# Attention block on one core: the opening rebuilt, from the loads to the first scores

## The chip, the core and the metric

The kernel runs on one core of a Trainium2 chip. The core has five engines with queues of their own: TensorE (PE in the profile; its weight loads are PEld), VectorE (DVE), ScalarE (ACT), GpSimd (POOL) and SyncE (SP), which here only issues DMAs. An engine takes its instructions in the order in which they were written; engines wait for each other by semaphores. TensorE writes its results to PSUM, eight banks of 128 partitions x 512 f32, which VectorE and ScalarE read. The metric is the device time of one execution in microseconds (us).

## The reference

Self-attention on x of 2048 x 448 with 16 heads of 28 channels, in bf16:

```python
qkv = (x @ wqkv).reshape(B, S, 3, H, Dh) ...   # B 1, S 2048, D 448, H 16, Dh 28
q, k, v = qkv[0], qkv[1], qkv[2]
scores = jnp.einsum("bhqd,bhkd->bhqk", q, k) * (Dh ** -0.5)
p = _softmax(scores, axis=-1)
o = jnp.einsum("bhqk,bhkd->bhqd", p, v)
return o (heads joined) @ wo
```

The bulk is the exponential of 16 x 2048 x 2048 scores and the two matmuls on either side of it.

## The kernel before

**Tiling.** Heads go in 4 groups `g` of 4, each head padded to 32 partitions, so a group fills 128. Queries go in 4 chunks `c` of 512, keys in 16 tiles of 128. One group and one chunk make a *set*; there are 16. A set has 4 x 16 = 64 *half-tiles* of scores, 128 keys x 512 queries of one head.

**Two ways to exponentiate.** ScalarE takes two half-tiles at once from a pair of banks (`a0` or `a1`) and writes the tile `pt` (line 802); ten `pt` tiles go round. VectorE takes one half-tile from bank `d0` or `d1` and forms bits of bf16 numbers by adding a constant (`I`, line 817). Four such are a chain; two more operations over the chain add further constants (`J`, line 840), and three terms together, the second and third with copies of V scaled by constants (`VS`, line 466), approximate the exponential. Three chains go round. PV (line 900) multiplies `pt`, `I` and `J` with V into bank `o`, one set at a time. Every exponential is taken of a score less a bound for its query, which comes from the norm of that query times the largest norm of the keys; the bound travels as a spare row of Q and a row of ones in K.

**What is needed before the first scores.** x is loaded in 4 blocks of 512 rows (`xs`), transposed on TensorE in pieces of 128 x 112 (line 508) and copied to `XT`, one half by VectorE (515), one by ScalarE (517). Then, for the first group, K of each block is projected (line 230, 16 matmuls), squared (244), summed by head with a matrix of ones (`blockK`, line 310), and the maximum over keys taken (315). Q of the first chunk is projected and squared too, and its norm summed (381). A root by bit shifts (321, 386, 389) and a join (394) give `QA0`, from which the first scores (621) are made. Only then may the first exponential run. K is copied to `KA` by ScalarE (259) or VectorE (262). V of the first two groups is projected in pairs of key tiles (445) and copied to `VA` (454 ScalarE, 456 VectorE).

**Zero rows.** Q of a set is also laid out in two tiles `QP` of 128 partitions with zeros at the other heads' rows, so that two heads fit one matmul. There are 16 such tiles; the old kernel clears them by 16 DMAs from a tile of zeros (line 539), issued by SP in the opening. `VA` and `WO` are cleared by GpSimd (161, 163), which then issues the 16 loads of `WO` (166).

**The order.** The order on each engine is written by a planner when the kernel is built. It holds a list of operations for each of PE, ACT, DVE and SP with an estimated duration, what they need, which bank they acquire (`acq`) and release (`rel`) and a priority (`pri`, smaller first), and a clock `free` for each engine; it advances the engine whose clock is least and lets it take the best operation that is ready. The landing times of the loads are constants in it (lines 528 to 530). `do_s` places a pair of half-tiles for ScalarE and, where a `d` bank is free (`d_banks`), half-tiles for VectorE. `pick_pe` decides between scores, PV (`do_pv`), listed operations, and matmuls of zeros as a filler. The planner's estimates fix the order alone; at run time the semaphores decide.

**Banks.** `a0` and `a1` are two banks each, `d0`, `d1`, `o` and `m` one. In the main part `m` serves all projections, norms and output projections.

The old opening takes the transposed blocks through `a0` and `a1`, each block a pair of banks and one tile `XT`; the loads of the Q and V weights are issued by ScalarE from within its copies of blocks 1 and 2:

```python
def evac(hf):
    ...
        nc.scalar.copy(out=dst, in_=src)
        if b == 1:
            load_w(0, nc.scalar)
        if b == 2:
            load_w(2, nc.scalar)
```

## Time and profile before

| what | us |
|---|---|
| three runs | 380.9, 380.94, 385.8; median 380.94 |
| profiled execution | 381.23 |
| its span on the core | 379.2 |
| ScalarE busy | 359.0 (95%), 400 instructions |
| TensorE busy | 346.4 (91%) |
| VectorE busy | 341.9 (90%) |
| GpSimd busy | 20.0 (5%) |
| exponentials on ScalarE (line 802) | 376, 345.6 busy |
| half-tiles on VectorE (line 817) | 272, 180.0 busy |
| granted clock of TensorE | 0.999 |

376 exponentials of two half-tiles and 272 single ones make the 1024 half-tiles. Rows of a timeline give start, length, engine, line, operation, output and inputs, shapes, how many instructions were merged and, in brackets, how long the engine stood idle before and what released it. Rows of groups give, behind the bar, busy us and mean ns of one, and then the idle time before them. A mean length contains the overlap with the next instruction, so spacing of starts is the better measure of a stream. The span is counted on the core; the profiled execution's own time has 2.0 us more around it.

### The profile page before, as it was taken

How to read it: one execution, taken by the hardware profiler on the slowest of the kernel's cores; microseconds unless marked ns; L12 is line 12 of the kernel's file. 1: busy time of each engine (PE TensorE's matmuls, PEld its weight loads, DVE VectorE, ACT ScalarE, POOL GpSimd, SP SyncE). 2: the span in 40 equal slices, each digit the busy share in tenths (PEclk: the TensorE clock that was granted, in tenths of full speed). 3: DMA queues.
4: the chain of work that ended last, by engine and by line, in shares of the span. 5: the costliest groups of instructions: out<-in, count | busy, mean ns of one | idle time of the engine just before them, and what ended most of it. 6: DMA issues, size and time to landing. Idle time of an engine off the chain costs nothing.

```text
span 379.2 us, 8747 instructions
## 1 busy us (share of the span) xinstructions
PE 346.4 (91%) x3442; PEld 113.3 (30%) x3462; DVE 341.9 (90%) x655; ACT 359.0 (95%) x400; POOL 20.0 (5%) x47
## 2 busy tenths in 40 slices
PE   7879999999999999999789999989889899989974
PEld 3443322222333233232222222222222222222222
DVE  2499998999999999999899899899999999999943
ACT  2779999999999999999999999999999999999992
POOL 8830000000000000000000000000000000000000
PEclk9999999999999999999999999999999999999999
DMA  8930001011100000011000001000000011110101
GB/s 251 246 102 16 3 19 38 3 41 28 41 6 15 18 3 29 14 28 40 4 30 7 25 15 41 28 31 2 28 5 4 28 39 42 37 43 12 56 14 48
DMA packets 16082, 14.03 MB, mean 37 GB/s; under 512 B 6077, under 2 KB 13609, under 8 KB 16041
## 3 DMA queue, kind: packets, MB, share of 16 engines
q1 hardware_dynamic: 13704, 11.18, 9.8%
q10 hardware_dynamic: 1824, 1.89, 1.8%
q8 instruction: 27, 0.44, 0.5%
q0 software_dynamic: 512, 0.40, 0.5%
q14 instruction: 15, 0.11, 0.1%
HBM read 7.37 MB, written 1.96 MB: 25 GB/s over the span
## 4 chain that ended last, share of the span: by engine, by line
ACT 56%; PE 22%; issue 9%; DMA 6%; DVE 4%; SPq 2%; ACTq 0%; DVEq 0%
ACT pt L802 54%; PE a L621 9%; PE o L900 6%; PE m L230 3%; DMA rr<-scr 3%; PE m L445 2%; DMA WRAW<-in_wqkv_dram 2%; SPq L359 2%; DVE I L817 1%; DMA QP<-zero 1%; DVE QA L353 1%; DVE J L840 1%; DMA den<-o_sb 1%; ACT sq L244 0%; ACT XT L517 0%
## 5 line engine op out<-in xcount | busy, mean ns | idle before, releaser
L802 ACT ACTIVATE pt<-a 128x1024 bf16<-128x1024 f32 x376 | 345.6, 1183 | 1.5 <-PE d L621 1.1
L817 DVE TENSOR_SCALAR I<-d 128x512 int16<-128x512 f32 x272 | 180.0, 682 | 8.0 <-PE d L621 6.6
L621 PE MATMUL a<-QP,KA 32*128 32x512 bf16 (+1 forms) x742 | 144.9, 380 | 18.2 <-ACT pt L802 17.0
L900 PE MATMUL o<-pt,VA 128*32 128x512 bf16 x752 | 106.5, 385 | 0.5 <-ACT pt L802 0.5
L621 PEld LDWEIGHTS <-KA 32*128 32x128 bf16 (+1 forms) x1024 | 52.6, 91 | 155.8 <-issue 153.6
L621 PE MATMUL d<-QP,KA 32*128 32x512 bf16 x267 | 92.6, 384 | 0.2 <-DVE I L817 0.2
L840 DVE TENSOR_SCALAR J<-I 128x2048 int16<-128x2048 int16 x136 | 90.1, 684 | 0.4
L900 PE MATMUL o<-J,VS 128*32 128x512 bf16 x544 | 74.4, 385 | 0.3
L900 PE MATMUL o<-I,VA 128*32 128x512 bf16 x272 | 65.9, 385 | 0.6 <-issue 0.5
L230 PE MATMUL m<-XT,WRAW 112*32 112x512 bf16 x464 | 35.5, 384 | 0.5 <-ACT XT L517 0.3
L900 PEld LDWEIGHTS <-VA 128*32 128x32 bf16 x1024 | 23.9, 94 | 37.0 <-issue 36.7
L900 PEld LDWEIGHTS <-VS 128*32 128x32 bf16 x544 | 16.5, 94 | 16.4 <-issue 16.4
L445 PE MATMUL m<-WRAW,XT 112*128 112x224 bf16 x112 | 15.4, 261 | 0.0
L230 PEld LDWEIGHTS <-WRAW 112*32 112x32 bf16 x512 | 8.4, 94 | 16.0 <-issue 12.9
L445 PEld LDWEIGHTS <-XT 112*128 112x128 bf16 x128 | 10.2, 97 | 7.8 <-issue 6.3
L262 DVE TENSOR_SCALAR KA<-m,kmask,ones 128x512 bf16<-128x512 f32 x13 | 10.4, 803 | 2.1 <-ACT sq L244 1.9
L353 DVE TENSOR_SCALAR QA<-m,qmask 128x512 bf16<-128x512 f32 x15 | 11.1, 742 | 0.5 <-PE m L230 0.5
L515 DVE COPY XT<-a 112x1024 bf16<-112x1024 bf16 x4 | 2.8, 692 | 9.4 <-ACT XT L517 7.8
L651 PE MATMUL o<-zero 128*128 128x512 bf16 x29 | 10.0, 384 | 1.3 <-issue 1.3
L481 PE MATMUL m<-WO,xs 128*128 128x448 bf16 x36 | 11.0, 359 | 0.0
L951 DVE TENSOR_TENSOR xs<-o_sb,rr 128x512 bf16<-128x512 f32 x12 | 8.2, 683 | 2.5 <-DMA rr<-scr 2.5
L929 DVE COPY o_sb<-o 128x512 f32<-128x512 f32 x15 | 10.3, 685 | 0.1
(104 smaller groups left out, 155.0 us busy)
## 6 DMA issues: line engine op xcount, KB each, us to landing
rr<-scr SPq DMA_DIRECT2D x15, 256.0 KB
QP<-zero SPq DMA_DIRECT2D x16, 128.0 KB
QP<-QA SPq DMA_DIRECT2D x60, 28.0 KB
out_dram<-osb SPq DMA_DIRECT2D x14, 112.0 KB
xs<-in_x_dram SPq DMA_DIRECT2D x3, 448.0 KB
WRAW<-in_wqkv_dram ACTq DMA_DIRECT2D x3, 392.0 KB
QP<-su SPq DMA_DIRECT2D x30, 2.0 KB
xs<-in_x_dram ACTq DMA_DIRECT2D x1, 448.0 KB
```

The lines of the kernel that those rows point to most:

```text
L230: nc.tensor.matmul(out=ps[HP * i:HP * (i + 1), :], lhsT=WRAW[t][:, cc, h * Dh:h * Dh + HP], rhs=XT[c][:, cc, :], start=(cc == 0), stop=(cc ...
L262: nc.vector.tensor_scalar(out=KAt[(g, sc)][:], in0=src, scalar1=kmask[:, 0:1], scalar2=ones[:, 0:1], op0=ALU.mult, op1=ALU.add)
L353: nc.vector.tensor_scalar(out=t[:], in0=held[key][:, 0:QW], scalar1=qmask[:, 0:1], scalar2=None, op0=ALU.mult)
L445: nc.tensor.matmul(out=held[key][:, part * w:(part + 1) * w], lhsT=XT[b][:, cc, t * P:(t + 1) * P], rhs=WRAW[2][:, cc, h * w:(h + 1) * w], ...
L481: nc.tensor.matmul(out=held[key][:, 0:D], lhsT=otile(g, c)[:, tq * P:(tq + 1) * P], rhs=WO[:, g, :], start=(g == 0), stop=(g == G - 1))
L621: nc.tensor.matmul(out=out_ap, lhsT=KAt[(g, j // XB)][r, (j % XB) * P:(j % XB + 1) * P], rhs=q[r, :], start=True, stop=True, tile_position ...
L651: nc.tensor.matmul(out=cur["o"][:], lhsT=zero[:, 0:P], rhs=zero[:], start=False, stop=False, skip_group_check=True)
L802: nc.scalar.activation(out=pt[:], in_=ps[:], func=ACT.Exp, scale=LN2 / 128.0)
L817: nc.vector.tensor_scalar(out=dst, in0=pd[:], scalar1=BIAS, scalar2=0.0, op0=ALU.add, op1=ALU.max)
L840: nc.vector.tensor_scalar(out=r[:, w], in0=ch["I"][:, w], scalar1=float(SHIFT[k]), scalar2=None, op0=ALU.add)
L900: nc.tensor.matmul(out=o[HP * i:HP * (i + 1), :], lhsT=vt[:, gg, j % XB, HP * i:HP * (i + 1)], rhs=e["ap"], start=(SETMM[key] == 1), stop= ...
L929: nc.vector.tensor_copy(out=st["o_sb"][:], in_=o[:])
```

## The change

- The first x block is loaded in two halves, by SP and by ScalarE's queue; the Q and V weights are loaded by SP right behind the x blocks. No load is issued from within a copy any more.
- Each transposed block is two tiles `XT{b}_0` and `XT{b}_1` of two pieces each, through two separate banks (`d0`, `d1` or `o`, `m`). ScalarE copies the first half, VectorE the second.
- The 16 zero-row DMAs are replaced by memsets: eight by VectorE in the setup, eight by GpSimd after the join. GpSimd's clearing of the second half of `VA` and of `WO`, and the loads of `WO`, also move behind the join; GpSimd becomes an engine of the planner.
- `k_first` replaces `k_job` and `kn_first` for the first group. Banks: K0 in `a0`, K1 in `a1`, K2 in `d1`, K3 in `o`; norms in the second half of `a0` and `a1`, in `a0`, and in `m`. K0 and K1 are copied by ScalarE, and squared from the copy in SBUF, by GpSimd and by VectorE; K2 and K3 are squared by ScalarE from PSUM and copied by VectorE only after the join. The copy of the first Q and the first scaling of its norm move from VectorE to ScalarE.
- V pairs of the first set all go through bank `m`, none through `o`; they, and every other operation of low priority on `m`, wait for the last norm of K.
- In the main part, `m` may serve as a third bank for VectorE's half-tiles while no operation that wants it is ready within 1 us; and in the first set a ready listed operation goes ahead of PV.

```diff
-    XT = [big.tile([CK, CC, QW], BF16, name=f"XT{b}") for b in range(NXB)]
+    XT = [[big.tile([CK, CC // 2, QW], BF16, name=f"XT{b}_{k}") for k in range(2)] for b in range(NXB)]
...
-    load_x(0, nc.sync)
+    load_x(0, nc.sync, 0, 2)
+    load_x(0, nc.scalar, 1, 2)
     load_w(1, nc.scalar)
     load_x(1, nc.sync)
     load_x(2, nc.scalar)
     load_x(3, nc.sync)
+    load_w(0, nc.sync)
+    load_w(2, nc.sync)
...
+    for c in range(NQC):
+        for k in range(2):
+            nc.vector.memset(QP[c][k][0][:], 0.0)
...
+    for b in range(NXB):
+        clear_v(0, b)
...
+        if op.acq == "m" and op.pri > 5 and ("KN0", NQC - 1) not in evt:
+            return None
...
+    def k_first(sc, bank, nbank, eng, sq_eng, pri, late=False):
+        key = ("K", 0, sc)
+        nkey = ("KN0", sc)
+        last = sc == NQC - 1
+        uses = 1 + (sq_eng == "ACT") + (nbank is None)
...
+        def sq():
+            if sq_eng == "ACT":
+                act_square(key, kmask)
+            else:
+                t = new_sq(key)
+                (nc.gpsimd if sq_eng == "POOL" else nc.vector).tensor_tensor(
+                    out=t[:], in0=KAt[(0, sc)][:], in1=KAt[(0, sc)][:], op=ALU.mult)
...
+        add("PE", CC * D_WAVE + 0.02, mm, pri=pri, cols=448 * CC, acq=bank,
+            need=[("XT", sc, 0), ("XT", sc, 1), ("W", 1)], gives=[key + (0,)])
+        add(eng, 0.72 if eng == "DVE" else 0.72, evac, need=[key + (0,)] + ([("QA", 0, 0)] if late else []), gives=[key],
+            rel=rel, pri=5 if late else pri)
...
             if first:
-                nc.vector.tensor_scalar(out=t[:], in0=held[key][:, 0:QW], scalar1=qmask[:, 0:1], scalar2=qoff[:, 0:1],
-                                        op0=ALU.mult, op1=ALU.add)
+                nc.scalar.activation(out=t[:], in_=held[key][:, 0:QW], func=ACT.Identity, bias=qoff[:, 0:1],
+                                     scale=qmask[:, 0:1])
...
+        def scaled():
+            held["z0"] = wk.tile([P, QW], BF16, name="z", bufs=1)
+            nc.scalar.mul(out=held["z0"][:], in_=held.pop("qn0")[:, 0:QW], mul=MARG ** 4)
...
+    def xt_job(b, banks, pri):
+        def tr(hf):
+            held[("xt", b, hf)] = bank_tile(banks[hf])
...
-    for n, t in (("x", 0), 5.4), (("W", 1), 5.6), (("x", 1), 7.2), (("x", 2), 9.0), (("x", 3), 10.3), \
-            (("W", 0), 13.0), (("W", 2), 14.8):
+    for n, t in (("x", 0), 5.0), (("W", 1), 6.3), (("x", 1), 8.1), (("x", 2), 9.4), (("x", 3), 10.3), \
+            (("W", 0), 11.6), (("W", 2), 13.0):
...
-            nc.sync.dma_start(out=QP[c][k][z][:], in_=zero[:])
+            nc.gpsimd.memset(QP[c][k][1][:], 0.0)
...
+    for c in range(NQC):
+        evt[("QZ", c, 0)] = (6.0, "DVE")
+        add("POOL", 1.1, lambda c=c: clear(c), need=["QN00"], gives=[("QZ", c, 1)], pri=10 + c)
+    for b in range(NXB):
+        add("POOL", 1.3, lambda b=b: clear_v(1, b), need=["QN00"], gives=[("VZ", b)], pri=20 + b)
+    add("POOL", 1.7, lambda: nc.gpsimd.memset(WO[:], 0.0), need=["QN00"], gives=["WOz"], pri=30)
+    for h in range(H):
+        add("POOL", 0.6, lambda h=h: load_wo(h), need=["WOz"], gives=[("WO", h)], pri=31 + h)
+    for b in range(NXB):
+        xt_job(b, ("d0", "d1") if b % 2 == 0 else ("o", "m"), 0.1 * b)
+    k_first(0, "a0", None, "ACT", "POOL", 2.0)
+    k_first(1, "a1", None, "ACT", "DVE", 2.1)
+    k_first(2, "d1", "a0", "DVE", "ACT", 2.2, late=True)
+    k_first(3, "o", "m", "DVE", "ACT", 2.3, late=True)
+    q_job(0, 0, "d0", QPRI, split=1)
+    qn_first("a1", 2.25)
...
-        v_job(0, kt, "o" if kt in (0, 4) else "m", 7 + kt, eng="ACT" if kt < 6 else "DVE")
+        v_job(0, kt, "m" if kt in (0, 4) else "m", 7 + kt, eng="ACT" if kt < 6 else "DVE")
...
     def d_banks(t):
-        return sorted((b for b in ("d0", "d1") if res[b] is not None and res[b] <= t + D_SOON), key=lambda b: res[b])
+        out_ = sorted((b for b in ("d0", "d1") if res[b] is not None and res[b] <= t + D_SOON), key=lambda b: res[b])
+        if len(out_) < 2 and res["m"] is not None and res["m"] <= t and len(a_fifo) < 2:
+            soon = [ready(op) for op in ops["PE"] if op.acq == "m"]
+            if not any(r is not None and r <= t + 1.0 for r in soon):
+                out_.append("m")
+        return out_
...
-        if pv_ok and (backlog >= 3 or last_chance or not op_ok):
+        if pv_ok and (backlog >= 3 or last_chance or not op_ok) and not (op_ok and op.pri < 40 and pts_used[0] < NPT):
```

More of the change, by code (lines that the diff above doesn't have):

```diff
@@ L1054, in pick_sp, with pick_pool @@
         return None, nxt
[L1056 removed]
+    def pick_pool(t):
+        op, nxt = best("POOL", t)
+        if op is not None:
+            return run(op, t), None
+        return None, nxt
+    pick = {"PE": pick_pe, "ACT": pick_act, "DVE": pick_dve, "SP": pick_sp, "POOL": pick_pool}
     stuck = 0
```

148 lines of the change are left out of this document (67 added, 81 removed).

## The prediction

> **What bounds the kernel now.** I read the page first (busy shares, groups), then the stretches of the exponential's line alone, then the waits, and last the order of time of the opening.
>
> ```profile
> span 379.2 us, 8747 instructions
> PE 346.4 (91%) x3442; PEld 113.3 (30%) x3462; DVE 341.9 (90%) x655; ACT 359.0 (95%) x400; POOL 20.0 (5%) x47
> ...
> L802 ACT ACTIVATE pt<-a 128x1024 bf16<-128x1024 f32 x376 | 345.6, 1183 | 1.5 <-PE d L621 1.1
> L817 DVE TENSOR_SCALAR I<-d 128x512 int16<-128x512 f32 x272 | 180.0, 682 | 8.0 <-PE d L621 6.6
> ...
> L840 DVE TENSOR_SCALAR J<-I 128x2048 int16<-128x2048 int16 x136 | 90.1, 684 | 0.4
> ```
>
> The stretches of line 802 alone (start:end, length, busy, number, clock, DMA share, GB/s), and one stretch of all engines (PE, PEld, DVE, ACT, POOL):
>
> ```profile
> 23.00:30.00 7.00, 6.39 (x7) 1.00 0.36 109
> 30.00:370.00 340.00, 339.08 (x370) 1.00 0.08 23
> 370.00:379.20 9.20, 0.00 (x0) 0.95 0.16 50
> ```
>
> ```profile
> 30.00:360.00 330.00, 309.98 (x3113) 96.30 (x3125) 316.68 (x572) 329.38 (x360) 0.00 (x0) 1.00 0.08 23
> ```
>
> So the time has three parts: 22.8 us before the first exponential (its row is below), some 347 us in which ScalarE runs exponentials without a gap (339.08 of 340), and some 9.4 us behind the last. In the middle part each exponential takes 339.08 / 370 = 0.916 us and does two half-tiles, 0.458 us each. VectorE does the rest of the half-tiles at (180.0 + 90.1) / 272 = 0.99 us each, and is idle for 330.00 - 316.68 = 13.3 us. The middle can get shorter only if VectorE takes half-tiles over: 1 us of its idle time filled is one half-tile, 0.458 us less of ScalarE, and since the end of both then comes nearer, 0.458 / 1.458 = 0.31 us of time. The opening is worth its length one for one.
>
> The chain of the opening (start, length) shows what it waits for at first, and the order of time how the rest goes:
>
> ```profile
> 0.73 6.17 DMA WRAW<-in_wqkv_dram
> ...
> 7.43 4.63 DMA QP<-zero
> ...
> 12.08 0.34 ACTq L112
> ```
>
> ```profile
> 5.65 1.39 PE L508 MATMUL a<-ident,xs 128*112 128x128 bf16 x16
> ...
> 7.07 1.01 ACT L517 COPY XT<-a 112x1024 bf16<-112x1024 bf16 x1 [4.05 <-PE a L508]
> ...
> 8.11 0.69 DVE L515 COPY XT<-a 112x1024 bf16<-112x1024 bf16 x1 [5.86 <-ACT XT L517]
> ...
> 8.53 1.10 PE L508 MATMUL a<-ident,xs 128*112 128x128 bf16 x16 [1.49 <-DMA xs<-in_x_dram]
> ...
> 9.56 1.05 PE L230 MATMUL m<-XT,WRAW 112*32 112x512 bf16 x16
> ...
> 10.54 0.96 PEld L508 LDWEIGHTS <-xs 128*112 128x112 bf16 x16 [0.42 <-issue]
> ...
> 16.82 1.05 PE L230 MATMUL a<-XT,WRAW 112*32 112x512 bf16 x16 [1.03 <-DMA WRAW<-in_wqkv_dram]
> ...
> 17.80 0.39 PE L310 MATMUL d<-sq,blockK 128*128 128x512 bf16 x1
> ...
> 18.12 1.05 PE L230 MATMUL o<-XT,WRAW 112*32 112x512 bf16 x16
> ...
> 19.28 0.69 ACT L244 ACTIVATE sq<-o,kmask 128x512 bf16<-128x512 f32 x1 [0.67 <-PE o L230]
> ...
> 20.02 0.38 PE L310 MATMUL d<-sq,blockK 128*128 128x512 bf16 x1 [0.53 <-ACT sq L244]
> ...
> 20.48 0.68 DVE L315 TENSOR_REDUCE kp<-d 128x1 f32<-128x512 f32 x1
> ...
> 21.58 0.75 DVE L394 SCALAR_TENSOR_TENSOR QA<-su,kroot,qt 128x512 bf16<-128x512 bf16 x1
> ...
> 22.82 2.85 ACT L802 ACTIVATE pt<-a 128x1024 bf16<-128x1024 f32 x3 [0.92 <-PE d L621]
> ```
>
> Three losses show. VectorE copies its half of the first transposed block only after ScalarE's (8.11 after 7.07 + 1.01). The load of the Q weights isn't issued before 12.08, behind a zero-row transfer, and Q's projection waits for it until 16.82. The last K projection starts at 18.12; from its end at 19.17 to the first exponential at 22.82 stand 3.65 us of square, norm, maximum, root, join and scores with hardly a gap.
>
> **The change part by part.**
>
> *Loads.* The seven loads of x and of the three weights (4 x 448 KB and 3 x 392 KB on the page, 3.04 MB) go out first; the twelve early zero-row transfers that ran among them go. The rates they had:
>
> ```profile
> 3.00:7.00 4.00, 3.99 (x23) 1.88 (x21) 0.00 (x0) 0.02 (x1) 3.77 (x9) 1.00 1.03 294
> 7.00:11.00 4.00, 2.51 (x41) 1.76 (x41) 0.98 (x2) 2.02 (x2) 3.83 (x8) 1.00 1.05 376
> ```
>
> That is 1.18 + 1.50 = 2.68 MB from 3 to 11 us, so all loads take till about 12 us and the Q weights, next to last, about 11: no longer the last thing awaited. The first x block comes on two queues; I take it 0.5 us earlier than 5.65 (between 0 and 1). The extra issue on ACT's queue (about 0.45 us) delays its table load, under the idle 4.05 us before 7.07; were that gone it would cost 0.45. SP issues two weight loads more and sixteen zero rows fewer.
>
> *Banks of their own.* Both copies of a block now run side by side. First block: transposes 5.15 to 6.5, VectorE's copy to about 7.25, ScalarE's from the first half sooner. K weights have landed at 6.90, so the first K projection runs 7.25 to 8.25, not 9.56, in time that PE idled.
>
> *The order after it.* PE's steps are 1.0 us a transposed block (9.56 to 8.53, 10.54 to 9.56 for a projection: 0.98) and 0.32 a norm (18.12 - 17.80). Blocks 1, 2, 3 by landing: 8.3, 9.8, 10.8, to 11.8; then K1, Q, K2, K3 at 0.98 and four norms between at 0.32, so K3 ends at 11.8 + 3.9 + 1.0 = 16.7, against 19.17 (one norm falls into the wait before block 2). Behind it the same 3.65: the first exponential at 20.3, **2.5 us earlier**. If blocks 2 and 3 land 1 us later: 1.5 us; if PE never waits: 5.15 + 1.39 + 3.0 + 4.9 + 1.3 + 3.65 = 19.4, 3.4 us, and 0.5 more if x lands sooner still. I take the middle.
>
> *Spread evacuations.* ScalarE gets the Q copy and the scaling of the norm, neither shown as such; the nearest rows are its K copy and its square (0.69 above):
>
> ```profile
> L259 ACT ACTIVATE KA<-m,ones,kmask 128x512 bf16<-128x512 f32 x1 | 0.8, 770 | 0.0
> L262 DVE TENSOR_SCALAR KA<-m,kmask,ones 128x512 bf16<-128x512 f32 x13 | 10.4, 803 | 2.1 <-ACT sq L244 1.9
> ```
>
> It gains 0.77 + 0.69 and loses two squares of 0.69: nothing. Its queue between 12 and 17.4 holds one K copy, three squares, the Q copy and the scaling, 0.77 + 2.07 + 0.77 + 0.69 = 4.3 us in 5.4, so K3's square waits 0 to 0.5 us; I take 0.2. One square goes to GpSimd, bounded by VectorE's rate and GpSimd's memset below at 0.5 to 2 us, off the path, as K0's norm isn't needed before 16. A second K copy (803 ns) moves behind the join, onto the busy VectorE: 0.8 x 0.31 = 0.25 us.
>
> *Memsets.* Eight zero rows on VectorE and, once the join is done, eight more, the second V half and the output weights on GpSimd:
>
> ```profile
> L144 DVE MEMSET maskK<- 128x256 uint32 x1 | 0.3, 272 | 0.0
> L161 POOL MEMSET VA<- 128x1024 bf16 x8 | 8.1, 1017 | 0.0
> ```
>
> ```profile
> 11.51 1.67 POOL L163 MEMSET WO<- 128x1792 bf16 x1
> ...
> 26.81 0.75 DVE L466 TENSOR_SCALAR VS<-VA 128x1024 bf16<-128x1024 bf16 x2
> ...
> 28.68 0.75 DVE L466 TENSOR_SCALAR VS<-VA 128x1024 bf16<-128x1024 bf16 x2
> ...
> 31.14 1.28 DVE L840 TENSOR_SCALAR J<-I 128x2048 int16<-128x2048 int16 x2
> ```
>
> VectorE: 8 x 0.272 = 2.2 us under its idle 5.86 before 8.11; uncovered it would delay the first copy. GpSimd: 8 x 0.51 + 4 x 1.02 + 1.67 with the small ones about 11 us, from 20 to 31, then the sixteen output-weight loads: all needed only sets later. I cost them at nothing; what that leaves out is the third rival.
>
> *V through one bank.* V pairs of the first set now all go through bank m, two of them went through o. Uses of m one after the other in the old first set:
>
> ```profile
> 30.74 0.62 PE L230 MATMUL m<-XT,WRAW 112*32 112x512 bf16 x8
> ...
> 34.38 0.56 PE L445 MATMUL m<-WRAW,XT 112*128 112x224 bf16 x4
> ...
> 39.88 1.08 SPq L425 DMA_DIRECT2D QP<-su  x2
> ...
> 42.65 0.56 PE L445 MATMUL m<-WRAW,XT 112*128 112x224 bf16 x4
> ```
>
> Between 30.74 and 42.65 lie four uses (Q1, V, norm, V), so 2.98 us each, 3.64 the longest. A set lasts 347 / 16 = 21.7 us, and from Q1's first matmul to the end of its rows' issue at 40.96 are 10.2. So Q1 has to start within 11.5 us of the first exponential (it was 7.9). Five V pairs stand before it; the first starts some 1.3 us ahead of the first exponential (the maximum that frees m ended at 20.48 + 0.68, 1.66 ahead). They fit if a use takes under 12.8 / 5 = 2.56 us. The matmuls of V now go ahead of PV's, and the first three pairs are copied by ScalarE, so I take 2.65: 0.45 us lost.
>
> *Third bank for VectorE's scores.* Where m is idle VectorE's next half-tile can be computed ahead. What it can remove is VectorE's wait for scores, 6.6 us on line 817 above; at most all 13.3 us of idle. I take half of 8.0: 4 x 0.31 = **1.25 us gained** (0 to 4.1; below nothing by up to 1 us if m then comes late to the projections).
>
> The sum against the profiled execution's 381.23: -2.5 + 0.2 + 0.25 + 0.45 - 1.25 = -2.85, so 378.4. The median shown, 380.94, is 0.3 lower, hence **378.1 us**. Its own range is 375.5 to 380.
>
> **The rivals.**
>
> *Bank m becomes the limit of the first set; ends slower.* For it speaks the mean of 2.98 us a use and that m is asked for by V, Q1 and the norm alike; against it that PE now prefers them. At 3.64 us a use Q1 starts 5 x 3.64 - 1.3 = 16.9 us after the first exponential, 5.4 too late, and ScalarE stands still for that time: 381.2 - 2.3 + 0.25 - 1.2 + 5.4 = 383.4, 383.1 on the median. From 3.2 us a use on the stall outweighs the rest (5 x 3.2 - 1.3 - 11.5 = 3.2).
>
> *The third bank fills VectorE.* All 13.3 us gone is 4.1 us, with an opening 3.4 earlier and no V loss: 381.2 - 3.4 - 4.1 + 0.25 = 374.0, 373.7 on the median and 373.2 with the earlier x. Against it: 5 of the idle 13.3 us don't stand before line 817.
>
> *GpSimd's memsets hold VectorE.* In the first 11 us of the old first set, to 33, VectorE ran four copies of V and two J (rows above). If each waits out half a 1.02 us memset, VectorE loses 3.1 us in an order that can't adapt: 378.4 + 3.1 = 381.5, 381.2 on the median, no change. The old trace has GpSimd's memsets over at 13.2 us and the first such operation at 26.8, so it can't tell. [...] No row before the change shows such a meeting.
>
> *The halves still wait for each other, or the loads come no sooner.* Then K0 starts after block 1 as before and only the Q-weight wait (1.03) and some 0.25 us of bank wait go, 1.3 us for 2.5: 379.6, 379.3 on the median.
>
> **How the numbers follow.** Forecast 0.5; third bank 0.12; memsets 0.13; halves or loads 0.1; bank m 0.15. The range 373.5 to 384 leaves the outer end of the second and of the last out. Two per cent, about what a measurement of this kernel can tell from no change, is 7.6 us: below 373.3 only the best of the second (0.07), above 388.6 only a worse stall than worked out here, or an order in the long middle that leaves gaps (0.06); between them 0.87.
>
> **What would show it.** The first exponential at 20.3 (19.4 to 21.3); the first two XT copies overlapping; K0's projection near 7.2; Q's with no DMA wait; under 376 exponentials, over 272 I; line 802 with under 2.5 us of idle time. Wrong: exponentials waiting near 40 us for Q1's scores, J or VS rows longer while POOL is busy, or as many exponentials as before.

## The result and the profile after

| | before | after |
|---|---|---|
| median of 20 runs each | 383.26 us (379.9 to 388.16) | 379.61 us (377.49 to 383.27) |
| profiled execution | 381.23 | 379.65 |
| its span | 379.2 | 377.9 |
| first exponential starts | 22.82 | 23.21 |
| from there to the end of the last | 346.9 | 345.2 |
| exponentials on ScalarE / half-tiles on VectorE | 376 / 272 | 374 / 276 |

The ratio is 0.9922, with an interval of 0.9895 to 0.9948: a gain of 0.8%, small but clear of zero, and within two per cent. The forecast was 378.1 with a range of 373.5 to 384. Its size was right; what it is made of was not. The forecast took 2.5 us of its 2.85 from the opening, and the opening got 0.4 us longer. What was gained stands in the middle part.

One thing is needed to read the times: runs of one kernel differ with the mean clock that TensorE was granted (of the 68 runs of before beside the experiments, those at 0.999 or more took 379.4 to 381.5 us, apart from a single one of 679.29, and those at 0.984 or less 384.8 to 387.9), and the ratios leave out runs over 1.5% above the fastest of their kernel. The profiled run of before has 0.999, that of after 0.991; the two profiles differ by 1.6 us and the medians by 3.7, and the ratio, 3.0 us of 381, lies between.

The page of after, engines and groups (group columns: line, engine, operation, tiles, count, then busy us and mean ns, then idle time before it and its releaser):

```profile
span 377.9 us, 8807 instructions
PE 353.9 (94%) x3480; PEld 115.7 (31%) x3480; DVE 347.7 (92%) x668; ACT 357.6 (95%) x398; POOL 25.4 (7%) x56
...
L849 ACT ACTIVATE pt<-a 128x1024 bf16<-128x1024 f32 x374 | 344.0, 1150 | 1.7 <-PE a L663 1.1
L864 DVE TENSOR_SCALAR I<-d 128x512 int16<-128x512 f32 x246 | 163.1, 683 | 7.3 <-PE d L663 6.8
L887 DVE TENSOR_SCALAR J<-I 128x2048 int16<-128x2048 int16 x138 | 90.7, 686 | 0.3
L864 DVE TENSOR_SCALAR I<-m 128x512 int16<-128x512 f32 x30 | 20.5, 682 | 0.0
```

Line 849 is the old 802, line 864 the old 817. Thirty half-tiles came through the third bank `m`, and VectorE has four half-tiles more in all; two exponentials of ScalarE are gone (345.6 busy before, 344.0 now), in the part in which it runs without a gap. VectorE is busy for 347.7 us, 341.9 before; the 138 `J` are two more.

The opening of after in order of time (start, length; in brackets the idle time before and its releaser):

```profile
5.43 1.56 PE L546 MATMUL d<-ident,xs 128*112 128x128 bf16 x16
...
6.53 1.01 ACT L554 COPY XT<-d 112x1024 bf16<-112x1024 bf16 x1 [3.04 <-PE d L546]
...
7.03 0.69 DVE L552 COPY XT<-d 112x1024 bf16<-112x1024 bf16 x1 [2.48 <-PE d L546]
...
8.95 1.05 PE L238 MATMUL a<-XT,WRAW 112*32 112x512 bf16 x16 [1.96 <-DMA WRAW<-in_wqkv_dram]
...
11.68 1.84 PE L546 MATMUL d<-ident,xs 128*112 128x128 bf16 x16
...
14.55 1.05 PE L238 MATMUL d<-XT,WRAW 112*32 112x512 bf16 x16
...
17.15 1.04 PE L238 MATMUL o<-XT,WRAW 112*32 112x512 bf16 x16
...
18.30 0.69 ACT L252 ACTIVATE sq<-o,kmask 128x512 bf16<-128x512 f32 x1
...
18.66 1.29 DVE L342 TENSOR_REDUCE kp<-a 128x1 f32<-128x512 f32 x2 [0.47 <-PE a L337]
...
19.87 0.68 DVE L342 TENSOR_REDUCE kp<-m 128x1 f32<-128x512 f32 x1
...
20.13 1.67 POOL L583 MEMSET WO<- 128x1792 bf16 x1
...
20.84 1.10 DVE L427 TENSOR_SCALAR su<-z 128x512 int16<-128x512 int16 x1
...
21.98 0.75 DVE L432 SCALAR_TENSOR_TENSOR QA<-su,kroot,qt 128x512 bf16<-128x512 bf16 x1
...
23.21 1.94 ACT L849 ACTIVATE pt<-a 128x1024 bf16<-128x1024 f32 x2 [1.06 <-PE a L663]
```

The two copies of the first block overlap, and the Q projection (14.55) no longer waits for a load. But the first K projection starts at 8.95, only 0.6 us before the old one: now it waits for the K weights, which landed at 6.90 before. The chain of after has that load (start, length), until 8.91:

```profile
1.17 7.74 DMA WRAW<-in_wqkv_dram
```

While they were awaited, TensorE stood still, and then its clock fell. Stretches of after (length, busy us of PE, PEld, DVE, ACT, POOL, then granted clock, DMA share, GB/s):

```profile
3.00:7.00 4.00, 3.99 (x23) 2.26 (x21) 1.53 (x6) 0.96 (x2) 3.77 (x8) 1.00 1.05 352
7.00:9.00 2.00, 0.05 (x4) 0.05 (x8) 0.69 (x1) 0.54 (x1) 0.12 (x1) 1.00 1.06 318
...
10.00:11.00 1.00, 1.00 (x10) 1.00 (x11) 0.00 (x0) 0.78 (x1) 0.09 (x1) 0.50 1.13 260
...
12.00:13.00 1.00, 1.00 (x12) 1.00 (x12) 0.61 (x1) 0.30 (x2) 1.00 (x3) 0.50 0.11 27
...
24.00:26.00 2.00, 2.00 (x13) 0.76 (x12) 1.32 (x3) 2.00 (x5) 2.00 (x5) 0.50 0.39 100
...
30.00:360.00 330.00, 317.20 (x3153) 97.06 (x3151) 320.06 (x580) 329.40 (x359) 0.86 (x2) 1.00 0.08 24
```

From 10 to 13 us, and again at 24 to 26, the clock is 0.50 (by finer stretches from 9.89 to 13.30 and from 23.54 to 26.95); the block transposed at 11.68 took 1.84 us, where blocks took 1.10 before. In the long stretch VectorE's idle time is 330.00 - 320.06 = 9.9 us, against 13.3.

The last part of the opening is also longer: from K3's end (18.19) to the first exponential 5.02 us, against 3.65. K3's maximum (19.87) queues on VectorE behind two other maxima, about 0.4 us; and `su` (the root by bit shifts of the query's norm), 0.29 us long before and beside the chain, is now on it and takes 1.10, with GpSimd's memset of `WO` running beside it from 20.13 to 21.80.

### The profile page after: what moved, and what is told of

The parts are those of the page before. It is cut to its first block, busy times and chain, and to the rows that moved or that the text cites. A ratio compares the mean times of both kernels' runs of the same rounds, so it can differ in the third digit from the quotient of the medians.

```text
span 377.9 us, 8807 instructions
## 1 busy us (share of the span) xinstructions
PE 353.9 (94%) x3480; PEld 115.7 (31%) x3480; DVE 347.7 (92%) x668; ACT 357.6 (95%) x398; POOL 25.4 (7%) x56
## 3 DMA queue, kind: packets, MB, share of 16 engines
HBM read 7.37 MB, written 1.96 MB: 25 GB/s over the span
## 4 chain that ended last, share of the span: by engine, by line
ACT 49%; PE 34%; issue 10%; DVE 3%; DMA 2%; POOL 1%; ACTq 0%
ACT pt L849 48%; PE a L663 13%; PE o L947 10%; PE m L238 5%; DMA WRAW<-in_wqkv_dram 2%; PE m L484 2%; POOL QP L572 1%; DVE J L887 1%; PE m L520 1%; DVE I L864 1%; PE o L693 1%; PE m L446 1%; DVE kp L342 1%; ACT KA L318 0%; PE m L696 0%
## 5 line engine op out<-in xcount | busy, mean ns | idle before, releaser
L849 ACT ACTIVATE pt<-a 128x1024 bf16<-128x1024 f32 x374 | 344.0, 1150 | 1.7 <-PE a L663 1.1
L864 DVE TENSOR_SCALAR I<-d 128x512 int16<-128x512 f32 x246 | 163.1, 683 | 7.3 <-PE d L663 6.8
L663 PE MATMUL a<-QP,KA 32*128 32x512 bf16 (+1 forms) x738 | 144.2, 381 | 13.3 <-ACT pt L849 12.4
L947 PE MATMUL o<-pt,VA 128*32 128x512 bf16 x748 | 103.7, 385 | 0.2 <-ACT pt L849 0.2
L663 PE MATMUL d<-QP,KA 32*128 32x512 bf16 x242 | 78.9, 384 | 0.0
L947 PE MATMUL o<-J,VS 128*32 128x512 bf16 x552 | 72.4, 385 | 0.0
L947 PE MATMUL o<-I,VA 128*32 128x512 bf16 x276 | 60.9, 385 | 0.1
L238 PE MATMUL m<-XT,WRAW 112*32 112x512 bf16 x432 | 33.3, 385 | 0.0
L864 DVE TENSOR_SCALAR I<-m 128x512 int16<-128x512 f32 x30 | 20.5, 682 | 0.0
L484 PE MATMUL m<-WRAW,XT 112*128 112x224 bf16 x128 | 18.4, 274 | 0.8 <-DVE kp L342 0.8
L693 PE MATMUL o<-zero 128*128 128x512 bf16 x52 | 17.8, 387 | 0.0
L663 PE MATMUL m<-QP,KA 32*128 32x512 bf16 x30 | 11.5, 384 | 0.0
```

Source lines behind the costliest of these rows:

```text
L238: nc.tensor.matmul(out=ps[HP * i:HP * (i + 1), :], lhsT=WRAW[t][:, cc, h * Dh:h * Dh + HP], rhs=XT[c][cc // 2][:, cc % 2, :], start=(cc == ...
L484: nc.tensor.matmul(out=held[key][:, part * w:(part + 1) * w], lhsT=XT[b][cc // 2][:, cc % 2, t * P:(t + 1) * P], rhs=WRAW[2][:, cc, h * w: ...
L663: nc.tensor.matmul(out=out_ap, lhsT=KAt[(g, j // XB)][r, (j % XB) * P:(j % XB + 1) * P], rhs=q[r, :], start=True, stop=True, tile_position ...
L693: nc.tensor.matmul(out=cur["o"][:], lhsT=zero[:, 0:P], rhs=zero[:], start=False, stop=False, skip_group_check=True)
L849: nc.scalar.activation(out=pt[:], in_=ps[:], func=ACT.Exp, scale=LN2 / 128.0)
L864: nc.vector.tensor_scalar(out=dst, in0=pd[:], scalar1=BIAS, scalar2=0.0, op0=ALU.add, op1=ALU.max)
```

## The experiments

The theory after the result: (A) the opening lost its gain to the late K weights and to what their wait did to TensorE's clock; the time gained is the third bank's. The rivals: (B) the opening's length isn't what counts, since the first set takes it back, through bank `m` and GpSimd's memsets; (C) the whole difference lies in the clock of the runs. In the table the middle is the span less the first exponential's start and less 9.5 us behind the last. The ratios are to before on the same chip; e1 to e4, e5 to e8 and e9 to e12 ran on three chips, and after's is not on record, so that medians from different groups differ by the chips too, and where the two disagree the ratios are the safer guide. First exponential and middle are those of one profile each.

| run | median us | ratio, interval | profiled span | first exponential | middle |
|---|---|---|---|---|---|
| after | 379.61 | 0.9922, 0.9895 to 0.9948 | 377.9 | 23.21 | 345.2 |
| e1_w1_first | 377.85 | 0.9914, 0.9877 to 0.995 | 376.0 | 19.94 | 346.6 |
| e2_fill | 378.61 | 0.9941, 0.9897 to 0.9985 | 375.8 | 21.16 | 345.1 |
| e3_no_third | 380.65 | 0.9983, 0.9945 to 1.002 | 378.3 | 21.82 | 347.0 |
| e4_old_third | 378.88 | 0.9947, 0.9901 to 0.9993 | 376.1 | 22.16 | 344.4 |
| e5_wo_early | 379.11 | 0.9895, 0.9838 to 0.9952 | 377.7 | 21.58 | 346.6 |
| e6_w1_wo | 377.36 | 0.9838, 0.9782 to 0.9895 | 375.5 | 19.28 | 346.7 |
| e7_warm | 378.5 | 0.9894, 0.9849 to 0.994 | 378.1 | 20.06 | 348.5 |
| e8_v_o | 380.63 | 0.9977, 0.9936 to 1.0019 | 378.1 | 21.13 | 347.5 |
| e9_w1_split | 377.0 | 0.9888, 0.9862 to 0.9914 | 374.6 | 20.14 | 345.0 |
| e10_clear_early | 378.18 | 0.9913, 0.9885 to 0.994 | 376.0 | 20.13 | 346.4 |
| e11_both | 377.29 | 0.9899, 0.9873 to 0.9925 | 375.5 | 20.40 | 345.6 |
| e12_both_zeros | 377.28 | 0.9896, 0.9871 to 0.9921 | 375.3 | 20.11 | 345.7 |

**The K weights first.** The whole first x block goes on SP's queue, so that the K weights are the first load of ScalarE's.

```diff
-    load_x(0, nc.sync, 0, 2)
-    load_x(0, nc.scalar, 1, 2)
+    load_x(0, nc.sync)
     load_w(1, nc.scalar)
```

> The changed kernel with one edit: the first x block goes out whole on SP's queue again, so the K weights are first on ScalarE's queue. Theory A (the opening's gain is lost because the K weights land 2 us later than before, 8.91 us for 6.90, PE stands idle from 7.0 to 8.95 and its clock is then halved from 10 to 13): K weights land at 6.9 to 7.4, the first K projection starts near 7.4, granted clock 1.0 in 10 to 13, first exponential at 21.0 (20.3 to 21.8) for 23.21, time 2 us under the changed kernel. Rival B (the order behind the loads and GpSimd's memsets set the opening): the projection starts earlier but the first exponential stays at 22.6 to 23.4 and the time within 0.5 us.

The order of time and the stretches of this run:

```profile
7.31 1.05 PE L237 MATMUL a<-XT,WRAW 112*32 112x512 bf16 x16 [0.65 <-ACT XT L553]
...
17.33 1.02 POOL L167 MEMSET VA<- 128x1024 bf16 x1
...
17.63 0.87 DVE L426 TENSOR_SCALAR su<-z 128x512 int16<-128x512 int16 x1
...
18.47 1.69 POOL L582 MEMSET WO<- 128x1792 bf16 x1
18.54 0.75 DVE L431 SCALAR_TENSOR_TENSOR QA<-su,kroot,qt 128x512 bf16<-128x512 bf16 x1
...
19.94 1.94 ACT L848 ACTIVATE pt<-a 128x1024 bf16<-128x1024 f32 x2 [0.99 <-PE a L662]
```

```profile
7.00:18.00 11.00, 9.61 (x140) 5.84 (x140) 5.97 (x12) 7.64 (x11) 8.67 (x17) 1.00 0.43 126
20.00:26.00 6.00, 6.00 (x37) 2.50 (x36) 4.13 (x9) 5.81 (x9) 5.69 (x12) 0.50 0.24 58
```

K0 starts at 7.31, behind the copy and no longer behind a load; the clock is 1.00 to 18 us; the first exponential is 3.3 us sooner. So the place in the queue made the weights late. But the median fell by 1.8 us only, and the ratio by 0.0008, which is 0.3 us: the clock is 0.50 from 20 to 26, and the middle is 1.4 us longer than after's. That is rival B in part. (`su` is at 0.87 here, beside a memset of `VA`.)

**Zero matmuls while the weights are awaited.** Same loads as after; TensorE multiplies zeros between the first block and K0.

```diff
+                for _ in range(9):
+                    nc.tensor.matmul(out=t[:], lhsT=zero[:, 0:P], rhs=zero[:], start=True, stop=True)
```

> The changed kernel with nine matmuls of zeros (128x512, into bank o) on PE between the first block's transposes and the first K projection, in the time that PE idles for the K weights; loads as in the change. Tells the late weights from the halved clock. Theory A, clock part (the idle time lets the clock fall): K projection still near 9.0, granted clock 1.0 from 9 to 14, the transposes of blocks 1 to 3 take 1.0 us each instead of up to 1.84, first exponential at 21.6 (21.2 to 22.2). Rival (the clock falls whatever PE does there, or x lands too late for it to matter): clock 0.5 again and first exponential within 0.4 of 23.2.

```profile
8.70 1.05 PE L238 MATMUL a<-XT,WRAW 112*32 112x512 bf16 x16 [0.86 <-DMA WRAW<-in_wqkv_dram]
...
10.61 1.06 PE L546 MATMUL d<-ident,xs 128*112 128x128 bf16 x16
```

```profile
9.00:20.00 11.00, 9.62 (x141) 5.78 (x134) 6.16 (x12) 7.64 (x12) 9.11 (x18) 1.00 0.28 66
```

The weights still come late (8.70), the same transposes take 1.06 instead of 1.84, and the first exponential is at 21.16. That splits the opening's loss. From K0's start to the end of K3's projection after took 9.24 us and this run 7.67, so the halved clock cost 1.6 us; of the remaining 0.5 us K0 came 0.25 sooner and `su` took 0.88 for 1.10. The late weights themselves cost 1.2 (21.16 to 19.94).

How long TensorE stood idle doesn't alone decide whether the clock falls. It fell after 1.96 us in after and within an idle time of 2.19 us in e3, which has the same loads (from 8.31 to 11.73, and 9.19 us from K0's start to K3's end). It didn't fall after 0.86 us here, after 1.26 in e8, or after 3.16 in e5, again with the same loads:

```profile
9.11 1.05 PE L239 MATMUL a<-XT,WRAW 112*32 112x512 bf16 x16 [3.16 <-DMA WRAW<-in_wqkv_dram]
```

```profile
9.00:20.00 11.00, 9.81 (x141) 5.92 (x141) 5.75 (x11) 7.38 (x10) 8.75 (x16) 1.00 0.28 68
```

So e5 and e8, without any filling, have their first exponential at 21.58 and 21.13, as this run has. How these cases differ stands in the last section. In time the filling isn't shown to pay: the median is 1.0 us under after's, but the ratio is 0.9941 for 0.9922.

**Without the third bank, and the third bank alone.** First after with `d_banks` as before; then before with only the new `d_banks`:

```diff
+        if len(out_) < 2 and res["m"] is not None and res["m"] <= t and len(a_fifo) < 2:
+            soon = [ready(op) for op in ops["PE"] if op.acq == "m"]
+            if not any(r is not None and r <= t + 1.0 for r in soon):
+                out_.append("m")
```

> The changed kernel without the third bank for VectorE's half-tiles; the opening is untouched. Theory A (the middle got 1.7 us shorter by that bank): the first exponential stays at 23.2, exponentials 376 or 377 for 374, the time 1.3 to 2.3 us above the changed kernel, so about the same as or slightly above the kernel before. Rival C (the shorter middle comes from the new order of the first set): exponentials 374, time within 0.5 us of the changed kernel.

> The kernel before with only the third bank for VectorE's half-tiles added. Theory A: first exponential at 22.8 as before, 374 exponentials, some 1.7 us faster than the kernel before, ratio 0.9955 (0.993 to 0.998). Rival C: 376 exponentials and a ratio of 1.000.

The groups of the one without it, then of the one with it alone:

```profile
L845 ACT ACTIVATE pt<-a 128x1024 bf16<-128x1024 f32 x376 | 345.8, 1168 | 0.8 <-PE d L663 0.5
L860 DVE TENSOR_SCALAR I<-d 128x512 int16<-128x512 f32 x272 | 179.8, 685 | 6.7 <-PE d L663 5.4
```

```profile
L807 ACT ACTIVATE pt<-a 128x1024 bf16<-128x1024 f32 x374 | 343.6, 1179 | 1.2 <-PE d L621 0.9
L822 DVE TENSOR_SCALAR I<-d 128x512 int16<-128x512 f32 x250 | 165.6, 684 | 6.6 <-PE d L621 5.7
...
L822 DVE TENSOR_SCALAR I<-m 128x512 int16<-128x512 f32 x26 | 17.8, 684 | 0.1
```

Without it 376 exponentials and the middle of before (347.0), and no gain that the interval can tell from none. (Its first exponential, forecast at 23.2, came at 21.82 though nothing in the opening was changed: `su` took 0.29 us here.) Alone, on the old opening, 374, a middle of 344.4, a median 0.7 us under after's and, by the ratio, a gain of 2.0 us where after has 3.0, with overlapping intervals: most of the change's gain is to be had from the third bank, and the rest is too small for these runs. Its price in exponentials is 345.8 - 344.0 = 1.8 us, or 345.6 - 343.6 = 2.0.

**The memset of `WO` moved into the setup**, away from `su`:

```diff
+    nc.gpsimd.memset(WO[:], 0.0)
...
-    add("POOL", 1.7, lambda: nc.gpsimd.memset(WO[:], 0.0), need=["QN00"], gives=["WOz"], pri=30)
+    evt["WOz"] = (9.7, "POOL")
```

> The changed kernel with GpSimd's memset of WO moved to its setup, where it idles from 7 to 11 us; the clearing of the second V half stays and then runs from 15.6 to 20.3. In the changed kernel the 128x512 int16 operation that makes su took 1.10 us (0.29 before) and ended 0.14 us after that memset. Lock theory (GpSimd's memset holds VectorE's fast operations): su takes 0.3 us wherever no memset of GpSimd overlaps it, or else ends with the one that does; with su free the first exponential comes 0.7 us earlier than the changed kernel's at equal start of K0. Rival (su is slow for another reason, its input or its place): su still near 1.1 us with no memset beside it. Time 0 to 0.8 us under the changed kernel.

`su` took 0.85 us, now beside a memset of `VA` (19.14 to 20.17) that took the place of `WO`'s. In six runs `su` stretches to some 0.15 us past the end of whichever memset it met: 21.94 for 21.80 (after), 18.50 for 18.35 (e1), 19.90 for 19.75 (e2), 20.31 for 20.17 here, and so in e8 and e9. The first exponential comes 1.6 us sooner than after's, but not by `su`: the clock stayed at 1.00 in the opening (above). The median is 0.5 us under after's, less than the scatter of six runs settles.

**Both, and `VA`'s clearing behind the loads of `WO`.** The K weights first, `WO` early, the second half of `VA` cleared last (`pri=60`).

> The changed kernel with the K weights first on ScalarE's queue, the WO memset in the setup and the clearing of the second V half put behind the loads of WO, so that no GpSimd memset lies near su. Lock theory: su 0.29 us, first exponential at 19.3 (19.0 to 19.7) for 19.94 with the K weights first alone; GpSimd's V memsets then fall at 23 to 28 us, where VS or J beside them stretch by up to 1 us each. Rival: su 0.9 again, first exponential at 19.9. Time 0.3 to 0.8 us under that of the K weights first alone, unless the stretched VS and J give it back.

```profile
17.73 0.28 DVE L427 TENSOR_SCALAR su<-z 128x512 int16<-128x512 int16 x1
...
19.28 1.94 ACT L849 ACTIVATE pt<-a 128x1024 bf16<-128x1024 f32 x2 [0.24 <-PE a L663]
...
21.57 0.97 POOL L167 MEMSET VA<- 128x1024 bf16 x1
...
21.81 2.32 DVE L505 TENSOR_SCALAR VS<-VA 128x1024 bf16<-128x1024 bf16 x2 [0.30 <-ACT VA L493]
...
22.66 1.19 POOL L167 MEMSET VA<- 128x1024 bf16 x1
```

With no memset beside it `su` is back at 0.28, and the first exponential is the earliest of all. But the memsets now meet the two copies of V, which take 2.32 us where they took 0.75. A `J` that meets the next memset (25.36) takes 1.49 us, and 0.68 at 27.36 (the 138 `J` of this run have a mean of 690 ns, those of after 686). So `su`, the copies of V and `J`, all TENSOR_SCALAR from SBUF to SBUF, are shown with and without a memset beside them: `su` 0.43 to 1.10 us and 0.28, the two copies 2.32 and 0.75, `J` 1.49 and 0.68; `su` ended some 0.15 us behind the memset it met (above), the two copies 0.28 behind the second of theirs (24.13 for 23.85). It isn't so for every operation in SBUF: the join `QA`, which reads two tensors, took 0.75 us in e1 beside the memset of `WO` (rows above) and 0.75 here without one, and `kroot`, a TENSOR_SCALAR of 128x1, took 0.15 us in after beside the memset of `WO` (at 20.77) and 0.15 here without one. What sets the held operations apart from the others no run shows. The clock stayed at 1.00 from 20 to 28 us in this run, and ScalarE still stood idle for about 1.7 us in its first 30 us of exponentials, 0.5 of it at the change of sets, so the halved clock isn't the only thing that takes the start back.

The second fall of the clock goes with a late `su`. In the profiles of after, e1, e2, e5 and e8 the first scores waited 1.01 to 1.26 us for the join, and the clock was then 0.50 for 3.4 to 10.2 us; in e3, e6, e9 and e11 they waited 0.44 to 0.59 and it stayed at 1.00; e10 is an exception (0.44, and 0.50 from 22.55 to 25.96). The wait alone doesn't decide it: in before and e4, with `su` at 0.29, the first scores waited 1.17 us and the clock stayed at 1.00. With the clock halved for 3.4 us or not at all (after, e2, e9) the middle is 345.0 to 345.2; halved for 6.8 (e1, e5) it is 346.6. So a memset beside `su` seems to cost more than the 0.6 to 0.8 us by which it holds `su`; no run changes that wait alone.

**Zeros in the last part of the opening**, four behind the norm of Q and six behind the first V pair, to see whether the second fall of the clock is what e1 lost:

```diff
+            if (h, kt, part) == (0, 0, 1):
+                zeros(6)
...
+    add("PE", 0.22 * 4, lambda: zeros(4), need=["qn0"], gives=["fill2"], acq="d0", rel="d0", pri=2.26)
```

> As the kernel before in this list, with ten matmuls of zeros on PE in its idle time between the last norm and the first scores (four behind Q's norm, six behind the first V pair). With the K weights first the granted clock was halved from 19 to 26 us, after PE had stood idle for half of 16 to 19. Clock theory: clock 1.0 throughout the first 30 us in most runs, the V matmuls of the first set 0.93 us a pair instead of 1.5 to 1.67, runs closer together, time 1 to 2 us under the kernel without the zeros. Rival (ScalarE's stream absorbs the slow matmuls, or the clock falls anyway): time within 0.4 us of it.

A miss. The zeros ran until 19.7 and held the first scores back to 19.63, from 18.85; the median is 1.1 us above e6's. Clock and delay aren't separated by it, and couldn't be: e6, its base, had the clock at 1.00 there already (mean clock 1.0 in five of its six runs).

**Two V pairs through `o` again**, on after:

```diff
-        v_job(0, kt, "m" if kt in (0, 4) else "m", 7 + kt, eng="ACT" if kt < 6 else "DVE")
+        v_job(0, kt, "o" if kt in (0, 4) else "m", 7 + kt, eng="ACT" if kt < 6 else "DVE")
```

> The changed kernel with two V pairs of the first set through bank o again. The prediction's reading (five V pairs through m delay Q1 by little, 0.45 us lost): Q1's projection starts 1 to 3 us sooner than 12.7 us after the first exponential, and the time falls by 0 to 0.6 us. Rival (PV is held up by V in its bank o, which the K3 copy also holds until after the join): time 0.5 us or more above the changed kernel.

Stretches around the change from the first set to the second, thirty us behind the start of each first set, in after and then in this run, and of this run its first set too (columns as above; ACT is the fourth).

```profile
43.20:53.20 10.00, 9.56 (x99) 3.70 (x97) 9.59 (x21) 9.52 (x11) 0.00 (x0) 1.00 0.00 1
```

```profile
22.00:30.00 8.00, 8.00 (x43) 3.50 (x41) 5.98 (x13) 5.55 (x8) 8.00 (x16) 0.50 0.27 58
41.10:51.10 10.00, 9.93 (x108) 3.30 (x107) 9.72 (x20) 10.00 (x12) 0.00 (x0) 1.00 0.02 5
```

With `o` Q1's projection starts 10.1 us after the first exponential (at 31.22), 2.6 sooner than in after, and the 0.48 us gap at the change of sets is gone (10.00 of 10), as forecast. But the time is the rival's, 1.0 us above after's by the median: in the first 8 us of the first set ScalarE is busy for only 5.55, with the clock at 0.50 in all of them. The one bank for V costs its 0.5 us and is still the better choice by these runs (ratio 0.9977 for 0.9922); how much of this loss is PV waiting for `o` and how much the clock, the run doesn't tell.

**The K weights in two halves, one behind each half of the first x block:**

```diff
-    load_w(1, nc.scalar)
+    load_w(1, nc.sync, 0, 2)
+    load_w(1, nc.scalar, 1, 2)
```

> The changed kernel with one edit: the K weights are loaded in two halves, one behind each half of the first x block, on both queues at once; x's other blocks come behind them. If the K weights are late in the changed kernel because on ScalarE's queue they share with x blocks on SP's: they land at 6.0 to 6.8, K0 starts at 6.7 to 7.2, when the copies of the first block are done, the first exponential at 20.0 (19.5 to 21.0), time 377.7 (377.0 to 378.5), as with the K weights first on their queue or a little better. If the loads are limited by their total or by their start alone: K0 still at 8.4 or later and time within 0.5 us of the changed kernel.

```profile
7.59 1.14 PE L240 MATMUL a<-XT,WRAW 112*32 112x512 bf16 x16 [0.26 <-ACT XT L556]
...
20.14 1.94 ACT L851 ACTIVATE pt<-a 128x1024 bf16<-128x1024 f32 x2 [0.38 <-PE a L665]
```

```profile
7.00:20.00 13.00, 10.75 (x150) 6.37 (x148) 7.43 (x14) 8.51 (x13) 10.25 (x19) 1.00 0.43 117
20.00:24.00 4.00, 3.37 (x34) 2.02 (x33) 3.70 (x7) 3.86 (x6) 3.69 (x7) 1.00 0.23 54
```

This is near to after as the forecast had imagined it: weights in time, clock at 1.00 throughout in this profile, first exponential at 20.14 (forecast 20.3), 374 exponentials, a middle of 345.0. That 20.14 is so near 20.3 is in part luck: K3's projection ends at 15.78 where the forecast had 16.7, and from there to the first exponential it takes 4.36 us where the forecast had 3.65. The run has the shortest span, 374.6, and the lowest median, 377.0, 2.6 us under after's (1.3 by the ratios).

**All clearing in the setup**, on e1 (`WO`, both halves of `VA`, all zero rows; K0 squared by VectorE so that GpSimd is free); then **this with e9's loads**; then **zeros added to that**, four and two:

```diff
+    nc.gpsimd.memset(WO[:], 0.0)
+    for b in range(NXB):
+        clear_v(1, b)
+    for c in range(NQC):
+        for k in range(2):
+            (nc.vector if c < 2 else nc.gpsimd).memset(QP[c][k][1][:], 0.0)
...
-    k_first(0, "a0", None, "ACT", "POOL", 2.0)
+    k_first(0, "a0", None, "ACT", "DVE", 2.0)
```

> The changed kernel with the K weights first on ScalarE's queue and all memsets of GpSimd and VectorE in the setup (the first square of K then by VectorE), so that they are over at 16.5, before su and before the first VS; beside them the loads of WO alone. Lock theory, from the run with V's second half cleared at 22 to 27 us, where a pair of VS took 2.32 us for 0.75 and ScalarE lost 1.5 us by 34 us: su 0.28, VS pairs 0.75, first exponential at 19.3, time 375.9 (375.2 to 376.8) where the clock stays whole, 377 where it is halved in the first set. Rival (the first set can't use an earlier start, whatever GpSimd does): time 377.4 or more.

> Both: K weights in halves on both queues and all memsets in the setup. First exponential at 19.0 (18.5 to 19.6), time 375.6 (374.8 to 376.8), the fastest of all; rival as for the one before, 377.4 or more.

> As the one before, with six matmuls of zeros in PE's idle time behind the norms (four, then two), which end before the join does. Clock theory: more of its runs at a whole clock than of the one before, first exponential not later than 0.2 us, time 0 to 1 us under it. Rival (the clock is decided elsewhere): same times, or 0.3 us more for the zeros.

The first two forecasts missed, and the times (378.18 and 377.29) are close to the rival's 377.4 or more. `su` is at 0.28 and the V copies at 0.76, so nothing meets a memset any more; but the first exponential comes at 20.13 and 20.40, not at 19, because TensorE now waits for blocks of x:

```profile
9.67 1.10 PE L554 MATMUL d<-ident,xs 128*112 128x128 bf16 x16 [0.69 <-DMA xs<-in_x_dram]
...
11.31 0.66 PE L554 MATMUL o<-ident,xs 128*112 128x128 bf16 x8 [0.54 <-DMA xs<-in_x_dram]
```

(e11; e1 and e9 had no such wait in these places.) Why these blocks are waited for when only memsets moved is open; in e11 TensorE also got to them sooner, its K0 starting at 6.68 for 7.59 in e9. The zeros of the last run left the median where it was (377.28 for 377.29); its six runs all have a clock of 0.997 or more and lie within 0.75 us, where e11's six spread over 2.1. With six runs each, e6, e9, e11 and e12 can't be told apart: 377.0 to 377.4, 1.0 to 1.6% under before on their chips.

Rival C falls as far as the parts go: exponentials are counted, not timed. The clocks on record tell against it for the whole too: at a mean clock of 0.991 to 0.993 seven runs of before took 381.9 to 384.0 us and seven of after 378.6 to 380.8, about 2.6 us less by the medians; at 0.999 or more, five runs of e4 took 377.7 to 378.7, where before's took 379.4 to 381.5. What lowers the mean clock of before to 0.98 in some runs no profile here shows.

## Why the prediction was right in sum and wrong in its parts

*Loads, and "K weights have landed at 6.90, so the first K projection runs 7.25".* This step failed. The 6.90 was read from the old trace, where the K weights were first in ScalarE's queue; the change puts half of the first x block in front of them. They landed at 8.91, K0 ran at 8.95. The forecast's own remark that all loads together take till about 12 us was right, and no help: it spoke of the sum and not of the order. That the queue place did it is shown (e1, e9; K0 starts at 8.42 to 9.11 in the five runs with the loads of the change, at 6.68 to 7.59 in the seven with others). By itself it wouldn't have missed the forecast's opening: with the weights as late and the clock whole, K3's projection ends at 16.23 to 16.81 (e2, e5, e8), where the forecast had 16.7. The 2.9 us by which the first exponential was late are the two steps that follow: 1.5 in front of K3's end (18.19), 1.4 behind it. That the weights then share the DMA engines with x blocks 1 and 3 of the other queue, which come in longer pieces (3584 bytes for 896 in after's trace; from 6 to 8.9 us the packets of the two queues took 53% and 52% of the engines' time), is argued only as a cause. "x 0.5 us sooner" was nearly right, 5.43 for 5.65.

*PE's steps of 1.0 and 0.32.* Taken from a trace with the clock at 1.00 throughout. Behind the wait for the weights the clock was halved from 10 to 13 us. No rival had it, though the forecast made room for a TensorE that waits. It cost about 1.6 us, more than the late weights themselves, and did not come in every profile with these loads (in after and e3, not in e5 and e8).

*"Behind it the same 3.65".* It was 5.02. The forecast moved the scaling of Q's norm to ScalarE and priced that queue (0.2; K3's square came 0.11 after its projection, as before, so nothing was lost), but not the new order behind it: TensorE computes Q's norm behind K3's (19.40 after 19.04), ScalarE waits 0.83 us for it, so `su` falls behind the root on VectorE instead of beside it (0.3), and the maxima of K1 and K2 now stand ahead of K3's (0.4). The remainder, 0.7 to 0.8, is `su` beside the memset (1.10 us for 0.29); in the runs with `su` at 0.28 or 0.29 (e3, e6, e10 to e12) this stretch takes 4.20 to 4.22.

*Memsets, and "about 11 us, from 20 to 31".* Wrong in time and in place. The planner's condition that they come after Q's norm fixes where they stand in GpSimd's order but makes no wait, so they ran from 11.9 to 21.8, ahead of the join (21.98) and not behind it. The rival was right in kind: beside a memset `su` took 1.10 us for 0.29, 0.8 us more. But it was `su`, not J and the V copies, which the rival priced at 3.1 us and which met none here (in e6 they did: 1.49 us for 0.68, 2.32 for 0.75). That each of them waits out half a memset was the author's assumption, and no run shows the 3.1 us; the runs showed `su` held for 0.15 to 0.8 us and, in e6, two V copies for 1.6.

*Banks of their own, Q's wait, the K copy behind the join.* The halves overlap and Q waits for nothing, as forecast. The late K copy (0.25) was not measured by itself.

*V through one bank.* Forecast 0.45, measured 0.48 as one gap, by the mechanism named: Q1's first matmul ran at 35.88, 12.7 us after the first exponential where the limit was put at 11.5, and ScalarE waited once at the change of sets:

```profile
46.98 1.94 ACT L849 ACTIVATE pt<-a 128x1024 bf16<-128x1024 f32 x2 [0.48 <-PE d L663]
```

*Third bank.* Forecast 1.25 from 4 us of idle time filled. VectorE took exactly four half-tiles more (272 to 276) and its idle time fell by 3.4. The count was right and the price was not: at 0.31 each, the price assumed that ScalarE's end and VectorE's move towards each other; measured is 1.8 to 2.0, 0.45 to 0.5 each, which is ScalarE's own 0.458. ScalarE alone sets the length of the middle, and VectorE's added time is taken from its idle time.

*The sum.* On the profiled pair it goes: the opening with ScalarE's queue, forecast -2.3, measured +0.4; the middle, forecast 0.25 + 0.45 - 1.25 = -0.55, measured -1.7; around the span, 0.3 less than before. That is -1.6 for -2.85. The middle's 1.7 is ScalarE's work alone (346.26 us busy in it before, 344.56 after, for two exponentials fewer); it stood idle for 0.64 us of it in both, so the gap at the change of sets was made up by less idle time elsewhere. That the median came so near the forecast is due to two errors of opposite sign, and to the clock of before's runs, which the medians and the ratio hold and the profiled pair doesn't. The rivals "halves or loads not sooner" (379.3) and "memsets" (381.2) came nearest to what happened, the first for a reason it didn't give.

## What to carry to other kernels

When loads are put in a new order, work out the landing of each from what now stands in front of it in its queue; a landing time read from the old trace belongs to the old order (6.90 there, 8.91 in the new one). A wait of TensorE is worth more than its length if the clock falls behind it (1.6 us more here): look at the granted clock in the microseconds after each wait. If the wait can't go it can be filled, but time it: one filling here kept the clock at 1.00 from 9 to 20 us in the profile (e2), another held the scores back from 18.85 to 19.63 (e7). Where one engine runs without a gap, a piece of work taken from it is worth its full length there, so long as the receiving engine has idle time; test such a part alone, as it may be most of the gain.

## What the runs showed of the hardware

- TensorE's clock was halved (0.50) for 3.4 us in after, from 9.89, after an idle time of 1.96 us (before 8.95), and from 20 to 26 us in e1, after idle times of 0.82 us (before 17.39) and 1.03 us (before 19.34); 0.86 us in e2 (before 8.70), 3.16 us in e5 (before 9.11) and 1.49 us in the kernel before (at 8.53) left it at 1.00. The eight stretches at 0.50 in the openings and first sets lasted 3.4 us (after twice, e2, e3, e10), 6.8 (e1, e5) or 10.2 (e8), one, two or three times the 3.41 us of the first, and the two falls in after (9.89 and 23.54) lie four times 3.41 us apart. Counted back from a fall in windows of that length, TensorE was busy for 39 to 49% of the window ahead of the fall in seven of the eight; the exception is e10, with 70%. All other such windows of 61% or more at 1.00 kept the clock, and so did one of 47% in e5. At other places a low share kept it too: 44% in e4 (18.35 to 21.76), 50% in before (19.00 to 22.41). So the place of the idle time seems to count, in windows that are the author's reading of the lengths: after's 1.96 us lie in one (43% busy), e5's 3.16 us are split between two (47% and 61%), and e2's zeros leave none under 75% up to 17.87. What makes the clock fall isn't shown beyond this, nor what lets it rise again: one window of work was enough in after, not in e1.
- An int16 operation of 128x512 on VectorE took 0.28 to 0.29 us alone and 0.43 to 1.10 beside a GpSimd memset, ending some 0.15 us after it in six runs; in e3, where it began 0.06 us before the end of a memset of 128x1024, it took 0.29. The join of two tensors kept its 0.75 us beside one (e1), `kroot` of 128x1 its 0.15 (after). VectorE's copies from PSUM kept their 0.69 us beside memsets (13.55 in after).
- More bytes a second didn't bring the awaited load sooner: 352 GB/s from 3 to 7 us after, 294 before, and the K weights 2.0 us later.
